# Attention, token mixer and two MLPs on one core: small VectorE operations rewritten one column at a time

## The chip, the cores and the metric

The kernel runs on one core of a Trainium2 chip. A core has five engines that work side by side, each through its own list of instructions in order: TensorE (PE in the rows; its weight loads are PEld), VectorE (DVE), ScalarE (ACT), GpSimd (POOL) and SyncE (SP), which here issues the DMA transfers. The metric is the time on the device in microseconds, median of several runs.

## What is computed

The reference is a block-causal attention, then a token mixer and a channel MLP, then a second MLP behind a row normalization. Cut to what matters here:

```python
x = attention(q, k, v)                       # 4 x 576 rows of 512
u = x + token_mix(x)
x2 = u + relu(u @ moe_w_ch1) @ moe_w_ch2     # first MLP
mu  = mean(x2, axis=-1)                      # per row
var = mean((x2 - mu) ** 2, axis=-1)
xn  = (x2 - mu) / sqrt(var + 1e-06) * g_ln
out = x2 + relu(xn @ moe2_w_ch1) @ moe2_w_ch2
```

The MLP weights arrive as 64-bit floats. The kernel turns them into 32-bit floats, scales each matrix by a power of two, and splits weights and rows into two 16-bit planes; each product is then three 16-bit matmuls.

## The kernel before

Rows lie on the 128 partitions. The program has an attention stage (to about 240 us of the profile) whose steps stand in a table; after it `Mlps` works through the first MLP (to about 555 us), and `Pairs` through the second (from 527 us to the end), in three passes of 768 rows by four groups of hidden units. While the first MLP still runs, VectorE also decodes the weights of the second one (lines 945 to 952), ScalarE scales and splits them, GpSimd forms the sums and the low planes, and SP stores the planes to DRAM and loads them again for the passes.

From 240 us on a planner (`Plan`) sets the order at build time: each step has an engine, a cost and the steps it needs, and is emitted when its planned time comes. The costs in that table are constants of the program and are the same before and after. On the chip every engine then goes through its list in that order and waits on semaphores.

Three pieces of small work on VectorE belong to the change.

- `spread(s)` makes the maximum of a set of four weight blocks ready for `diagonal` (ScalarE, line 987) and `across` (TensorE, line 993). For ten of the sets it reduces four columns to one (line 968) and works on one column: line 975 masks and shifts, line 976 joins that with a bit of the original. For the four sets to which the gains `g_ln` belong it works on four columns (lines 979 to 981) and reduces at the end (line 982).
- `root()` adds the epsilon to the variances of two row blocks (line 1436, two columns), and ScalarE takes the square root (`power`, line 1439).
- `newton()` refines the inverse root: a reciprocal (line 1443) and four operations on two columns (lines 1444 to 1447). `normed` (line 1451) then normalizes 128 x 512 elements with the mean and the inverse root as scalars per partition.

There are nine such pairs of row blocks, three for each pass. Behind `normed`, GpSimd forms sums of rows (line 1459), ScalarE and GpSimd make the planes (lines 1475 and 1477), and SP issues the DMA that transposes them for TensorE (line 1481).

In the second MLP VectorE combines the results of the first product (lines 1583 to 1611, tiles mm, hid, u, h), makes the low planes (line 1594), and adds up the second product (line 1657, tile psy). TensorE's matmuls of the first product are line 1550, those of the second line 1637. Of the first MLP they are lines 1163 and 1196.

Of the kernel before, what the change touches and what calls it, by code (L numbers as in the profile page):

```python
# [14 lines left out]
I32 = mybir.dt.int32  # L15
AF = mybir.ActivationFunctionType
ALU = mybir.AluOpType
# [4 lines left out]
P = 128  # L22
# [764 lines left out]
class Mlps:  # L787
# [173 lines left out]
    def spread(self, s):  # L961

        nc, top = self.nc, self.mx[s]
        m1 = self.small([P, 1], "mx1", 3)
        g = self.gains(s)
        m = self.small([P, 4], "mxf", 3) if g else m1
        if not g:
            nc.vector.tensor_reduce(m1, top, axis=AX.X, op=ALU.max)
            top = m1
        mi, ti = m.bitcast(I32), top.bitcast(I32)  # L970
        if not g:
            t1 = self.small([P, 1], "mxt", 3)
            ti, m1 = m1.bitcast(I32), self.small([P, 1], "mxu", 3)
            mi = t1.bitcast(I32)
            nc.vector.tensor_scalar(mi, ti, 0x07FFFFFF, 3, ALU.bitwise_and, ALU.logical_shift_left)
            nc.vector.scalar_tensor_tensor(
                m1.bitcast(I32), ti, 0x40000000, mi, ALU.bitwise_and, ALU.bitwise_or)
        else:
            nc.vector.tensor_scalar(mi, ti, 0x07FFFFFF, 3, ALU.bitwise_and, ALU.logical_shift_left)
            nc.vector.scalar_tensor_tensor(mi, ti, 0x40000000, mi, ALU.bitwise_and, ALU.bitwise_or)  # L980
            nc.vector.tensor_tensor(m, self.ga4, m, ALU.mult)
            nc.vector.tensor_reduce(m1, m, axis=AX.X, op=ALU.max)
        self.mx[s] = m1

# [364 lines left out]
class Pairs:  # L1349
# [58 lines left out]
    def plan_rows(self, p, t):  # L1408
        m, nc, st, plan = self.m, self.nc, {}, self.m.plan
        js = (6 * p + 2 * t, 6 * p + 2 * t + 1)  # L1410
        if p == 0:
            a, x = (("xt0", "u1"), ("xr", "wt2"), ("xt0", "u1"))[t]
# [20 lines left out]
        def root():  # L1433
            va, st["r"] = m.small([P, 2], "va", 3), m.small([P, 2], "vr", 3)
            st["va"] = va
            nc.vector.tensor_scalar(va, st["mv"][:, :, 1], 1e-6, None, ALU.add)  # L1436

        def power():
            nc.scalar.activation(st["r"], st["va"], AF.Sqrt)

        def newton():
            va, r, t_ = st["va"], st["r"], m.small([P, 2], "vt", 3)
            nc.vector.reciprocal(r, r)
            nc.vector.tensor_tensor(t_, r, r, ALU.mult)
            nc.vector.tensor_tensor(t_, t_, va, ALU.mult)
            nc.vector.tensor_scalar(t_, t_, -2.0, 6.0, ALU.mult, ALU.add)
            nc.vector.tensor_tensor(r, r, t_, ALU.mult)

        def normed(i):
            x = st["x"][i]  # L1450
# [50 lines left out]
        for i in range(2):  # L1501
            add(f"stats{i}", "DVE", 0.9, lambda i=i: stats(i), *got[i])
        add("root", "DVE", 0.2, root)
        add("power", "ACT", 0.25, power, "root")
        add("newton", "DVE", 1.0, newton, "power")
        for i in range(2):
            add(f"normed{i}", "DVE", 0.5, lambda i=i: normed(i), "newton",
# [293 lines left out]
```

## Time and profile before

| | us |
|---|---|
| median of 3 runs | 913.77 (910.42 to 915.55) |
| the profiled execution | 907.16 |
| its span, first to last instruction | 905.4 |
| PE busy | 829.2 (92% of the span) |
| DVE busy | 736.2 (81%) |
| POOL busy | 513.9 (57%) |
| ACT busy | 503.7 (56%) |

The span is what the trace shows; 1.8 us of the execution lie around it. The mean granted clock of TensorE is 0.977 of full speed. Busy shares are means over stages with different limits, so the stages have to be read one by one.

### The profile page before, as it was taken

The page shows a single profiled execution, that of the slowest core. Times are in us where ns is not written, and L with a number is a line of the kernel's source. Part 1 is how long each engine was busy: PE and PEld are TensorE (multiplying, and loading weights), DVE is VectorE, ACT ScalarE, POOL GpSimd, SP SyncE. Part 2 cuts the span into 40 slices and gives each one's busy share as a digit, 9 for nine tenths or more (in the row PEclk, how much of TensorE's full clock was granted, in tenths as well). Part 3 has the DMA queues.
Part 4 walks back from the last instruction along what each step waited for, and adds up shares of the span by engine and source line. Part 5 has one row for each costly group of instructions (what it writes and reads, how often), then busy time and mean ns, then how long its engine had stood idle before and what let it go on. Part 6 is the DMA issues. An engine that isn't in the chain of part 4 may idle for free. (4 is left out here: it accounts for less than half of the span.)

```text
span 905.4 us, 18022 instructions
## 1 busy us (share of the span) xinstructions
PE 829.2 (92%) x6606; PEld 562.3 (62%) x6606; DVE 736.2 (81%) x1434; ACT 503.7 (56%) x1211; POOL 513.9 (57%) x505
## 2 busy tenths in 40 slices
PE   6778988889889999999999887998999899999995
PEld 4567877778744454445444353675777667777774
DVE  6999877989986887989899986689867787666776
ACT  6788886877665567555565544553434443344330
POOL 4778788598100345346658785486556654572224
PEclk9979998999899999999999999999999999999998
DMA  8999999999994732436546994659747667455522
GB/s 214 235 198 185 231 204 196 168 231 206 253 259 117 186 117 98 132 107 212 201 179 182 304 336 170 232 187 230 194 152 261 193 170 204 145 192 174 171 76 81
DMA packets 237993, 171.71 MB, mean 190 GB/s; under 512 B 184208, under 2 KB 204176, under 8 KB 237904
## 3 DMA queue, kind: packets, MB, share of 16 engines
q1 hardware_dynamic: 237904, 170.56, 70.9%
q8 instruction: 52, 0.85, 0.4%
q14 instruction: 37, 0.30, 0.1%
HBM read 102.50 MB, written 28.84 MB: 145 GB/s over the span
## 5 line engine op out<-in xcount | busy, mean ns | idle before, releaser
L1196 PEld LDWEIGHTS <-hid 128*128 128x128 f16 x648 | 63.3, 98 | 75.3 <-issue 1.0
L1196 PE MATMUL psy<-w,hid 128*128 128x512 f16 x432 | 95.7, 380 | 0.0
L1163 PEld LDWEIGHTS <-w 128*128 128x128 f16 x480 | 46.9, 98 | 52.4 <-issue 7.0
L1550 PEld LDWEIGHTS <-xr__4654 128*128 128x128 f16 x504 | 49.4, 99 | 34.8 <-issue 6.8
L1550 PE MATMUL mm<-big,xr__4654 128*128 128x384 f16 x336 | 64.8, 331 | 6.4 <-DVE hid L1583 4.3
L1561 POOL TENSOR_TENSOR acc<-u__4660,acc 128x384 f16<-128x384 f32 x36 | 32.9, 915 | 64.3 <-ACT acc L1557 64.2
L437 ACT ACTIVATE wide<-ps,nm 128x128 f32<-128x128 f32 (+3 forms) x128 | 65.8, 524 | 4.0 <-POOL hlA L461 2.0
L1550 PEld LDWEIGHTS <-wt__4653 128*128 128x128 f16 x504 | 49.2, 98 | 28.1 <-issue 3.7
L1550 PE MATMUL mm<-big,wt__4653 128*128 128x384 f16 x336 | 63.4, 326 | 3.3 <-DVE hid L1583 3.3
L1174 ACT ACTIVATE hid<-mm 128x512 f16<-128x512 f32 (+1 forms) x60 | 32.6, 549 | 53.7 <-PE mm L1163 53.5
L1637 PE MATMUL psy<-acc,acc 128*128 128x256 f16 x432 | 62.4, 273 | 0.0
L1203 POOL TENSOR_TENSOR acc<-acc,big 128x512 f32<-128x512 f32 x12 | 15.3, 1274 | 83.0 <-ACT big L1202 83.0
L461 POOL TENSOR_TENSOR hlA<-wide,hlA 128x1024 f16<-128x1024 f32 (+1 forms) x32 | 55.3, 1737 | 9.7 <-DVE hlA L457 6.8
L1557 ACT ACTIVATE xt<-mm 128x384 f16<-128x384 f32 x30 | 14.7, 490 | 80.9 <-DVE u__4660 L1611 64.4
L372 PE MATMUL ps<-kt 64*128 64x256 f32 (+3 forms) x384 | 51.7, 386 | 6.4 <-ACT wide L437 3.1
L414 DVE TENSOR_REDUCE mx<-ps 128x2 f32<-128x768 f32 (+3 forms) x64 | 50.5, 815 | 8.5 <-PE ps L377 8.4
L1637 PE MATMUL psy<-acc,xt 128*128 128x256 f16 x378 | 53.7, 273 | 3.1 <-ACT hid L1654 2.4
L1583 DVE TENSOR_TENSOR hid<-mm,hid 128x384 f32<-128x384 f32 x72 | 39.8, 552 | 17.4 <-PE mm L1550 11.6
L1637 PE MATMUL psy<-acc,w 128*128 128x256 f16 x378 | 50.1, 273 | 2.2 <-DVE w L1657 1.2
L1177 DVE SCALAR_TENSOR_TENSOR hid<-mm,hid 128x512 f16<-128x512 f32 (+1 forms) x60 | 37.3, 631 | 17.7 <-ACT hid L1174 17.4
L1637 PE MATMUL psy<-acc,wt__4655 128*128 128x256 f16 x324 | 44.8, 273 | 5.0 <-DVE big L1657 4.0
L1637 PEld LDWEIGHTS <-acc 128*128 128x128 f16 x432 | 42.2, 98 | 9.7
(288 smaller groups left out, 2326.6 us busy)
## 6 DMA issues: line engine op xcount, KB each, us to landing
raw<-in_moe_w_ch_dram SPq DMA_DIRECT2D x56, 512.0 KB, 3.9
acc<-w2d SPq DMA_DIRECT2D x84, 256.0 KB, 3.8
wt__4653<-w1d SPq DMA_DIRECT2D x12, 896.0 KB, 4.8
xr__4654<-w1d SPq DMA_DIRECT2D x12, 896.0 KB, 4.9
rawq<-in_q_dram SPq DMA_DIRECT2D x16, 256.0 KB, 3.2
rawq<-in_k_dram SPq DMA_DIRECT2D x16, 256.0 KB, 3.6
rawv<-in_v_dram SPq DMA_DIRECT2D x32, 128.0 KB, 3.7
u_dram<-u SPq DMA_DIRECT2D x8, 512.0 KB, 4.4
```

What stands on the lines that cost most here:

```text
L372: nc.tensor.matmul(views[hh], kt[r, a, KQ + t * P : KQ + (t + 1) * P], kt[r, c, KK : KK + n], start=i == 0, stop=False)
L414: nc.vector.tensor_reduce(s["mx"][:, c : c + 2], ps, axis=AX.X, op=ALU.max)
L437: nc.scalar.activation(d[:, g, sl], s["ps", key][:, g, sl], AF.Exp, scale=SCALE, bias=s["nm"][:, c + g : c + g + 1], accum_out=s["rs"][:, ...
L461: (nc.vector if last else on("l" + key)).tensor_tensor(lo_, src, hi, ALU.subtract)
L1163: self.nc.tensor.matmul(ps.rearrange("p (t n) -> p t n", n=P), W[:, a, h * P : (h + 1) * P], self.xt[b][:, :, 4 * c + k], start=i == 0, st ...
L1174: self.nc.scalar.activation(hid[:, 0, :w], ps, AF.Relu)
L1177: self.nc.vector.scalar_tensor_tensor(hid[:, 1, :w], ps, 0.0, hid[:, 0, :w], ALU.max, ALU.subtract)
L1196: self.nc.tensor.matmul(y, self.hid[v, h][:, a, k * P : (k + 1) * P], W[:, c], start=i == 0, stop=i == 11)
L1550: self.nc.tensor.matmul(ps[:, : self.W].rearrange("p (t n) -> p t n", n=P), w[:, i, j, a], x[:, :, at, j, c], start=first and n == 0, stop ...
L1561: self.nc.gpsimd.tensor_tensor(h[:, 1], src, h[:, 0], ALU.subtract)
L1583: add(k, "DVE", 0.55, lambda: dve.tensor_tensor(ps(src) if out is None else T[out], ps(src), T[x], ALU.add), 0)
L1637: self.nc.tensor.matmul(ps, h[:, a, t * P : (t + 1) * P], self.w2[o][:, r, c], start=n == 0, stop=n == 5)
```

## The change

Each of the small operations is written as one instruction per column, 128 x 1 elements. Where the other operand was a tensor it is now a scalar per partition, a column of a tile. Line 976 becomes a tensor_scalar whose second operand is the column. The four-column form gets a tile of its own for the shifted words (mxt4). In `newton` the square of r and its product with the variance become one instruction with two scalars per partition. The reciprocal and the reduction stay as they were.

```diff
@@ spread @@
             mi = t1.bitcast(I32)
             nc.vector.tensor_scalar(mi, ti, 0x07FFFFFF, 3, ALU.bitwise_and, ALU.logical_shift_left)
-            nc.vector.scalar_tensor_tensor(
+            nc.vector.tensor_scalar(
                 m1.bitcast(I32), ti, 0x40000000, mi, ALU.bitwise_and, ALU.bitwise_or)
         else:
-            nc.vector.tensor_scalar(mi, ti, 0x07FFFFFF, 3, ALU.bitwise_and, ALU.logical_shift_left)
-            nc.vector.scalar_tensor_tensor(mi, ti, 0x40000000, mi, ALU.bitwise_and, ALU.bitwise_or)
-            nc.vector.tensor_tensor(m, self.ga4, m, ALU.mult)
+            t4 = self.small([P, 4], "mxt4", 2)
+            cols = [[x[:, k : k + 1] for k in range(4)] for x in (ti, t4.bitcast(I32), mi, m)]
+            for t_, c, _, _ in zip(*cols):
+                nc.vector.tensor_scalar(
+                    c, t_, 0x07FFFFFF, 3, ALU.bitwise_and, ALU.logical_shift_left)
+            for t_, c, w, _ in zip(*cols):
+                nc.vector.tensor_scalar(w, t_, 0x40000000, c, ALU.bitwise_and, ALU.bitwise_or)
+            for k in range(4):
+                w = cols[3][k]
+                nc.vector.tensor_scalar(w, w, self.ga4[:, k : k + 1], None, ALU.mult)
             nc.vector.tensor_reduce(m1, m, axis=AX.X, op=ALU.max)
@@ root, newton @@
-            nc.vector.tensor_scalar(va, st["mv"][:, :, 1], 1e-6, None, ALU.add)
+            for i in range(2):
+                nc.vector.tensor_scalar(
+                    va[:, i : i + 1], st["mv"][:, i, 1:2], 1e-6, None, ALU.add)
...
-            va, r, t_ = st["va"], st["r"], m.small([P, 2], "vt", 3)
-            nc.vector.reciprocal(r, r)
-            nc.vector.tensor_tensor(t_, r, r, ALU.mult)
-            nc.vector.tensor_tensor(t_, t_, va, ALU.mult)
-            nc.vector.tensor_scalar(t_, t_, -2.0, 6.0, ALU.mult, ALU.add)
-            nc.vector.tensor_tensor(r, r, t_, ALU.mult)
+
+            nc.vector.reciprocal(st["r"], st["r"])
+            t2 = m.small([P, 2], "vt", 3)
+            cols = [[x[:, i : i + 1] for i in range(2)] for x in (st["va"], st["r"], t2)]
+            for va, r, t_ in zip(*cols):
+                nc.vector.tensor_scalar(t_, r, r, va, ALU.mult, ALU.mult)
+            for va, r, t_ in zip(*cols):
+                nc.vector.tensor_scalar(t_, t_, -2.0, 6.0, ALU.mult, ALU.add)
+            for va, r, t_ in zip(*cols):
+                nc.vector.tensor_scalar(r, r, t_, None, ALU.mult)
```

The lists of TensorE, ScalarE, GpSimd and SP are the same before and after, with the same waits. On VectorE only the instructions shown change. First, VectorE at a set with gains in the first MLP (lines 979 to 982 of before), with the neighbours on its list; L1177 and L1205 read TensorE's results. Before:

```order
L952 SCALAR_TENSOR_TENSOR raw_75<-raw_75,word 128x512
L1177 SCALAR_TENSOR_TENSOR hid_4391<-mm,hid_4391 128x512
L979 TENSOR_SCALAR mxf<-mx_6390 128x4
L980 SCALAR_TENSOR_TENSOR mxf<-mx_6390,mxf 128x4
L981 TENSOR_TENSOR mxf<-ga_4839,mxf 128x4
L982 TENSOR_REDUCE mx_6565<-mxf 128x1
L1205 SCALAR_TENSOR_TENSOR acc_3917<-psy,rs,acc_3917 128x512
```

The same place of VectorE's list now; the lines behind the change have higher numbers, so that 1184 is the old 1177 and 1212 the old 1205:

```order
L1184 SCALAR_TENSOR_TENSOR hid_4391<-mm,hid_4391 128x512
L982 TENSOR_SCALAR mxt_6587<-mx_6410 128x1 x4
L985 TENSOR_SCALAR mxf<-mx_6410,mxt_6587 128x1 x4
L988 TENSOR_SCALAR mxf<-mxf,ga_4839 128x1 x4
L989 TENSOR_REDUCE mx_6585<-mxf 128x1
L1212 SCALAR_TENSOR_TENSOR acc_3917<-psy,rs,acc_3917 128x512
```

Three instructions of four columns became twelve of one. Second, VectorE at the last pair of row blocks of the third pass, whose rows are made ready at 725 us of the profile: va is the variance, vr the inverse root, and the other rows combine TensorE's results. Before:

```order
L1657 SCALAR_TENSOR_TENSOR hid_4390<-psy,rg,hid_4390 128x512
L1436 TENSOR_SCALAR va<-mv 128x2
L1657 SCALAR_TENSOR_TENSOR hid_4391<-psy,rg,hid_4391 128x512
L1594 SCALAR_TENSOR_TENSOR wt__4655<-mm,wt__4655 128x384
L1443 RECIPROCAL vr<-vr 128x2
L1444 TENSOR_TENSOR vt<-vr 128x2
L1445 TENSOR_TENSOR vt<-vt,va 128x2
L1446 TENSOR_SCALAR vt<-vt 128x2
L1447 TENSOR_TENSOR vr<-vr,vt 128x2
L1583 TENSOR_TENSOR mm<-mm,hid_4386 128x384
```

The same place of VectorE's list now (1670, 1607 and 1596 are the old 1657, 1594 and 1583):

```order
L1670 SCALAR_TENSOR_TENSOR hid_4390<-psy,rg,hid_4390 128x512
L1444 TENSOR_SCALAR va<-mv 128x1 x2
L1670 SCALAR_TENSOR_TENSOR hid_4391<-psy,rg,hid_4391 128x512
L1607 SCALAR_TENSOR_TENSOR wt__4655<-mm,wt__4655 128x384
L1452 RECIPROCAL vr<-vr 128x2
L1456 TENSOR_SCALAR vt<-vr,va 128x1 x2
L1458 TENSOR_SCALAR vt<-vt 128x1 x2
L1460 TENSOR_SCALAR vr<-vr,vt 128x1 x2
L1596 TENSOR_TENSOR mm<-mm,hid_4386 128x384
```

One instruction became two at L1436, and four became six behind the reciprocal; their neighbours stand where they stood.

## Rows read from the trace of the kernel before

**Rows 1.** Page, part 2: busy tenths of PE in 40 slices of 22.6 us.

```profile
PE   6778988889889999999999887998999899999995
```

**Rows 2.** Windows, DVE on tiles mxf, vt, then L1436, L976: window, us, busy (count), ....

```profile
240.00:740.00 500.00, 7.94 (x16) 0.99 0.64 195
...
240.00:740.00 500.00, 15.51 (x36) 0.99 0.64 195
...
240.00:740.00 500.00, 5.92 (x9) 0.99 0.64 195
...
240.00:740.00 500.00, 5.25 (x10) 0.99 0.64 195
```

**Rows 3.** Timeline of POOL and DVE: start, us, instruction, [idle before it].

```profile
613.73 0.92 POOL L1561 TENSOR_TENSOR acc<-u__4660,acc 128x384 f16<-128x384 f32 x1 [0.76 <-ACT acc L1557]
613.75 0.15 DVE L1443 RECIPROCAL vr<-vr 128x2 f32<-128x2 f32 x1
613.94 0.72 DVE L1444 TENSOR_TENSOR vt<-vr 128x2 f32<-128x2 f32 x1
...
615.48 2.12 POOL L1477 TENSOR_TENSOR w<-u__4659,w 128x1024 f16<-128x1024 f32 x1
615.57 2.05 DVE L1446 TENSOR_SCALAR vt<-vt 128x2 f32<-128x2 f32 x1
```

**Rows 4.** One-column instructions: by tile (ns min/median/max), then timeline of DVE, POOL.

```profile
L975 DVE TENSOR_SCALAR mxt<-mx x10: 153/153/154, 240.7 to 561.5; 128x1 int32<-128x1 int32 x10
...
513.77 0.15 DVE L1001 TENSOR_SCALAR wi<-wt 128x1 int32<-128x1 int32 x1
...
513.85 0.14 DVE L1003 TENSOR_SCALAR ws<-wt 128x1 int32<-128x1 int32 x1
...
514.11 0.73 POOL L1460 TENSOR_TENSOR u__4660<-acc,acc 128x256 f32<-128x256 f32 x1
514.15 0.21 DVE L1026 TENSOR_SCALAR rg<-wi 128x1 f32<-128x1 f32 x1
```

**Rows 5.** Timeline of DVE, PE and ACT, 463 to 544 us.

```profile
463.58 0.69 DVE L1177 SCALAR_TENSOR_TENSOR hid<-mm,hid 128x512 f16<-128x512 f32 x1 [0.51 <-ACT hid L1174]
...
504.59 1.79 DVE L976 SCALAR_TENSOR_TENSOR mxu<-mx,mxt 128x1 int32<-128x1 int32 x1
...
506.87 0.22 PE L993 MATMUL mm<-diag,ones 128*128 128x128 bf16 x1 [2.46 <-ACT diag L987]
...
529.45 0.67 ACT L896 ACTIVATE raw<-raw 128x512 f32<-128x512 f32 x1 [3.38 <-DMA raw<-in_moe_w_ch_dram]
...
543.96 1.14 PE L1550 MATMUL mm<-big,wt__4653 128*128 128x384 f16 x6 [3.28 <-DVE hid L1583]
```

**Rows 6.** Windows: us, then busy of PE, PEld, DVE, ACT, POOL; PEclk, DMA, GB/s.

```profile
508.00:512.00 4.00, 4.00 (x12) 1.51 (x11) 3.23 (x10) 1.27 (x2) 0.59 (x1) 0.57 1.00 210
610.00:635.00 25.00, 20.52 (x156) 15.04 (x155) 22.77 (x42) 10.00 (x23) 15.18 (x16) 1.00 0.90 221
```

**Rows 7.** Timeline of DVE and PE around 562 us.

```profile
561.67 1.14 DVE L976 SCALAR_TENSOR_TENSOR mxu<-mx,mxt 128x1 int32<-128x1 int32 x1
...
563.33 2.99 PE L1550 MATMUL mm<-big,xr__4654 128*128 128x384 f16 x9 [3.16 <-DVE hid L1583]
```

**Rows 8.** Timeline of DVE: the normalization at 581 us, a product at 626 us.

```profile
581.37 0.90 DVE L1451 TENSOR_SCALAR x__4657<-x__4657,mv,vr 128x512 f32<-128x512 f32 x1
...
626.74 2.05 DVE L1445 TENSOR_TENSOR vt<-vt,va 128x2 f32<-128x2 f32 x1
```

**Rows 9.** Timeline of DVE and PE, 708 to 734 us.

```profile
708.74 1.58 DVE L1444 TENSOR_TENSOR vt<-vr 128x2 f32<-128x2 f32 x1
...
717.97 0.82 PE L1637 MATMUL psy<-acc,wt__4655 128*128 128x256 f16 x6 [1.02 <-DVE big L1657]
...
725.71 2.06 DVE L1436 TENSOR_SCALAR va<-mv 128x2 f32<-128x2 f32 x1
...
733.73 1.15 PE L1550 MATMUL mm<-raw,xr__4654 128*128 128x384 f16 x6 [0.92 <-DVE xt L1594]
```

## The prediction

> **What bounds the kernel now.** I read the slices of the page first, then the waits of TensorE, then the timeline of VectorE and GpSimd at the lines of the change. The slices show that TensorE is at nine tenths or more from 270 to 500 us and again from 725 us nearly to the end; between them it falls to 7 or 8 tenths in a few slices, at 498 to 566, 611 to 634 and 701 to 724 us [rows 1]. Only there can a faster VectorE shorten the program: in the full stretches a stall on VectorE is covered by matmuls. So the worth of the change has to be read place by place, not from VectorE's busy time.
>
> Next, the small operations. Their lines are busy for 7.94, 15.51, 5.92 and 5.25 us, 34.62 us in 71 instructions [rows 2]. That is 0.49 us each, for one to four columns. A one-column operation on the same engine takes 153 to 154 ns in all ten cases [rows 4]. Had all 71 taken 0.155 us they would be busy 11.0 us, so 23.6 us are stall. The timeline shows what they stall on: the reciprocal at 613.75 us starts while GpSimd runs and takes 0.15 us; the tensor_tensor behind it, also on two columns, ends at 614.66 us, with GpSimd's instruction (613.73 + 0.92 = 614.65); the tensor_scalar at 615.57 us lasts 2.05 us and ends at 617.62 us, again just as GpSimd does (615.48 + 2.12 = 617.60) [rows 3]. Reading: operations with two tensors from SBUF, and tensor_scalars from SBUF to SBUF on two columns, wait until GpSimd's running instruction ends; others pass.
>
> **The change part by part.** It makes all of these one column wide, with scalars for second tensors. A one-column tensor_scalar with constants has no stall in ten cases. With a scalar from a tile there is a case right under a running GpSimd instruction (514.11 to 514.84 us): line 1026 at 514.15 us takes 0.21 us [rows 4]. I take it that the new forms do not wait, and that all 23.6 us go.
>
> Added are 63 instructions: three in each of the 9 norm sets, nine in each of the 4 sets with gains. Two operations that don't need each other start 0.08 us apart (513.77 and 513.85) [rows 4]; one that needs the result before it starts 0.19 us after it (613.75 and 613.94) [rows 3]. So 63 cost 5.0 to 12.0 us. Columns of one step don't need each other, so I take 5.0. A scalar from a tile costs 0.06 us more (0.21 against 0.15) [rows 4]; there are 6 such reads per norm set, 8 per set with gains, and 10 at line 976: 96, or 5.8 us. Together 10.8 us on VectorE (bounds 5.0, if the reads are hidden, and 17.8), against 23.6 gone. Per norm set it is 0.6, per set with gains 1.2, at line 976 0.06 us.
>
> There is a rule that speaks against such a rewrite. The Trainium skill, page "VectorE: DVE Perf Modes", section "The DRAIN you can't avoid", says that after every operation the pipeline is flushed before the next one starts, and the page's rules advise to keep the number of operations small. The two starts 0.08 us apart, with the first lasting 0.15 us, don't agree with a full flush between independent operations. By the rule the addition would be the upper end, 17.8 us, and places 3 to 5 below would lose about 0.3 us each.
>
> What of it lies on TensorE's path, in five places; durations are those of the profiled execution:
>
> *Place 1, 504 us.* TensorE waits 2.46 us at 506.87 for the diagonal that ScalarE builds from line 976, which lasted 1.79 us [rows 5]. Here 1.79 - 0.16 - 0.06 = 1.57 us go. VectorE has had no idle time since 463.58 us [rows 5] and in that stretch passed one set with gains, two norm sets and another root. At the mean stalls of rows 2 (1.4 per set with gains, 1.1 per norm set behind the reciprocal, 0.5 per root) that is 5.1 us, less 2.6 added: at least the 0.9 us missing from 2.46. So the wait goes whole. Behind it TensorE was granted 0.57 of its clock over 508 to 512 us [rows 6], part of it at 1.2 instead of 2.4 GHz, right after that idle stretch; 4 x 0.43 = 1.7 us more. Upper end 4.2 us. But TensorE's next wait, 3.28 us at 543.96, is for VectorE, behind ScalarE that stood 3.38 us at 529.45 for a weight load from DRAM [rows 5], with the DMA engines at a share of 1.00 [rows 6]. If that load comes no earlier, all of the 4.2 us becomes a longer wait there. Lower end 0. Some of the transfers ahead of the load hang on VectorE's normalization and do move; I take 2.0.
>
> *Place 2, 562 us.* TensorE waits 3.16 us for a product that stands right behind line 976 on VectorE, 1.14 us long [rows 7]. 1.14 - 0.16 - 0.06 = 0.9 us go. The upper end is 2.3, if the wait shortens enough that the slow matmuls behind it (9 in 2.99 us, against 6 in 1.14 at 543.96 [rows 5, 7]) run at speed; lower 0.5. I take 0.9.
>
> *Place 3, 610 to 635 us.* TensorE is idle for 25 - 20.52 = 4.5 us [rows 6]. VectorE stalls 0.72 - 0.16 and 2.05 - 0.16 us in one norm set [rows 3], 2.05 - 0.16 in the next [rows 8]. The first of these is only half won: behind the norm set stands line 1451, from SBUF to SBUF on 512 columns, which waits for GpSimd too (0.90 us at 581.37 [rows 8]), and GpSimd runs until 617.60 [rows 3]. I count 1.3 us for the first set (its products, line 1657, do move ahead) and 1.9 - 0.6 = 1.3 for the second: 2.6. Bounds 1.3 and 4.5.
>
> *Place 4, 708 to 718 us.* 1.58 - 0.16 - 0.6 = 0.8 us on VectorE, with a wait of TensorE of 1.02 us behind it [rows 9]: 0.8, bounds 0.3 and 1.0.
>
> *Place 5, 726 to 734 us.* The root is 2.06 us long; ScalarE's square root and what stands behind that wait for it. 2.06 - 0.16 - 0.08 less 0.6 for the set behind it is 1.2 us, of which TensorE's wait of 0.92 us [rows 9] can give 0.9; bounds 0.3 and 0.9.
>
> Elsewhere the stalls are covered by matmuls [rows 1] and worth nothing. The sum is 2.0 + 0.9 + 2.6 + 0.8 + 0.9 = 7.2 us, with ends at 0 + 0.5 + 1.3 + 0.3 + 0.3 = 2.4 and 4.2 + 2.3 + 4.5 + 1.0 + 0.9 = 12.9. After 735 us TensorE is full [rows 1], so what it has gained by then should reach the end. The profiled execution took 907.16 us, 6.6 below the median of 913.77; 7.2 us from the median give 906.6.
>
> **The rivals.**
>
> *Hidden after all.* Place 1 turns wholly into a longer wait at 544, and the others give their lower ends: 2.4 us, 911.4. For it: the load at 529 and the full DMA engines; each engine waits for the others in these stages. Against: at places 2, 4 and 5 the waiting instruction stands directly behind the stalled one.
>
> *All of it.* The load moves with VectorE, and the clock stays up behind places 1 and 2: 11 us or more, 902.8. For it: 2.46 us is a short wait, and VectorE has several us in hand before 504.
>
> *A scalar read waits as a tensor does.* If one column with a scalar from a tile waits for GpSimd, the change doesn't do what it says, and it waits more often: eight times instead of two in a set with gains, four times instead of three behind a reciprocal. At a mean stall per operation of (7.94 - 16 x 0.155) / 12 = 0.46 and (15.51 - 36 x 0.155) / 36 = 0.28 us [rows 2], a set with gains stalls 3.7 instead of 1.4 us, a norm set 1.1 as before less the 0.5 of the root, and 1.2 and 0.6 us of added work come on top. A set with gains is then 3.5 us longer; the one in the stretch up to 504 makes TensorE's wait there longer by about that, and the norm sets at places 3 to 5 are 0.1 us longer each: about 4 us and with the slow clock behind it 5, 918.8. It decides from the first case in which line 1456 or 1460 lasts as long as GpSimd's instruction. Against it: line 1026 [rows 4], but that is a single case.
>
> **How the numbers follow.** Forecast, some 5 to 9.5 us gained: 0.48, alone 904 to 909. All of it: 0.17. Hidden: 0.28. The scalar that waits: 0.05; something else that costs as much: 0.02. A measurement here can tell 0.5%, 4.6 us, from no change. Faster by more than that: 0.65, the first two. Within it: 0.28. Slower: 0.07. The range reaches from 902 (all of it, less a little) to 912.5 (hidden, with the spread of the runs).
>
> **What would show it.** Right: lines 982 to 988, 1444 and 1456 to 1460 at 0.15 to 0.27 us each, none as long as a GpSimd instruction; no wait of TensorE at line 1000 near 504; the waits at 563, 717 and 733 us and the idle time of 610 to 635 us shorter or gone; line 1464 (the old 1451) longer than before in some cases, since it now meets GpSimd. Wrong: a wait near 541 longer by what 504 gained; any of the new lines at 0.5 us or more.

## The result and the profile after

The changed kernel takes 899.31 us (median of 4 runs, 898.71 to 900.28), the kernel before beside it 914.39 (4 runs, 910.42 to 915.55): a ratio of 0.9844 with a 95% interval of 0.9814 to 0.9873. It is faster, as forecast, but by some 15 us instead of 7.2, and below the range. The two profiled executions, 907.16 and 900.28 us, lie only 6.9 us apart. So two things have to be found: whether each part did what was forecast, and where the other 8 us come from.

TensorE's totals and slices of the page after, which answer to [rows 1]:

```profile
PE 828.0 (92%) x6606; PEld 562.9 (63%) x6606; DVE 721.8 (80%) x1497; ACT 503.0 (56%) x1211; POOL 514.0 (57%) x505
...
PE   6778988888799999999999997899999999999995
```

The slices at 611 to 634 and 701 to 724 us, which stood at 8, 9 and 9, 8, are full; the dip at 540 to 565 us is still there.

The timeline of VectorE and GpSimd at the place of [rows 3]:

```profile
613.50 0.91 POOL L1574 TENSOR_TENSOR acc<-u__4660,acc 128x384 f16<-128x384 f32 x1 [0.77 <-ACT acc L1570]
613.52 0.15 DVE L1452 RECIPROCAL vr<-vr 128x2 f32<-128x2 f32 x1
613.71 0.46 DVE L1456 TENSOR_SCALAR vt<-vr,va 128x1 f32<-128x1 f32 x2
614.09 0.27 DVE L1458 TENSOR_SCALAR vt<-vt 128x1 f32<-128x1 f32 x2
614.27 0.33 DVE L1460 TENSOR_SCALAR vr<-vr,vt 128x1 f32<-128x1 f32 x2
614.38 0.91 POOL L1574 TENSOR_TENSOR w<-h__4656,w 128x384 f16<-128x384 f32 x1
614.52 0.74 DVE L1670 SCALAR_TENSOR_TENSOR hid<-psy,rg,hid 128x512 f32<-128x512 f32 x1
615.18 2.47 DVE L1464 TENSOR_SCALAR x__4658<-x__4658,mv,vr 128x512 f32<-128x512 f32 x1
615.25 2.12 POOL L1490 TENSOR_TENSOR w<-u__4659,w 128x1024 f16<-128x1024 f32 x1
```

GpSimd runs from 613.50 on, and VectorE passes under it: the set takes 614.52 - 613.52 = 1.00 us. In seven of the nine sets it is 1.00 to 1.01 us; behind the other two, at 507 and 577 us, VectorE stands idle before its next instruction. What waits now is the normalization, line 1464 (the old 1451), 2.47 us beside GpSimd's 2.12, as the prediction said.

Windows of VectorE, for tiles mxf and vt and lines 1444 and 976 as in [rows 2], and line 982, which now writes another tile:

```profile
240.00:740.00 500.00, 4.83 (x36) 0.98 0.65 197
...
240.00:740.00 500.00, 8.02 (x54) 0.98 0.65 197
...
240.00:740.00 500.00, 2.24 (x18) 0.98 0.65 197
...
240.00:740.00 500.00, 2.14 (x10) 0.98 0.65 197
...
240.00:740.00 500.00, 1.29 (x16) 0.98 0.65 197
```

Together 18.5 us in 134 instructions, against 34.6 in 71. The waits of TensorE from 300 to 740 us (what, for whom: us, times, longest):

```profile
PE mm L1563 <- DVE hid L1596: 7.9, 5, 3.0
PE psy L1650 <- ACT hid L1667: 2.3, 4, 0.8
PE mm L1563 <- DVE xt L1607: 2.1, 2, 1.1
PE psy L1650 <- DVE big L1670: 0.6, 1, 0.6
PE psy L1650 <- DVE hid L1670: 0.2, 1, 0.2
```

The wait for the diagonal, 2.46 us [rows 5], is gone. Its place is taken in part by what was feared. The timeline of TensorE:

```profile
505.84 0.22 PE L1000 MATMUL mm<-diag,ones 128*128 128x128 bf16 x1
...
538.72 1.14 PE L1563 MATMUL mm<-big,wt__4653 128*128 128x384 f16 x6 [1.77 <-DVE hid L1596]
542.84 2.08 PE L1563 MATMUL mm<-big,wt__4653 128*128 128x384 f16 x6 [2.98 <-DVE hid L1596]
...
563.48 2.84 PE L1563 MATMUL mm<-big,xr__4654 128*128 128x384 f16 x11 [2.23 <-DVE hid L1596]
```

And of ScalarE ahead of it:

```profile
528.63 0.67 ACT L896 ACTIVATE raw<-raw 128x512 f32<-128x512 f32 x1 [5.27 <-DMA raw<-in_moe_w_ch_dram]
```

ScalarE now stands 5.27 us for the weight load instead of 3.38, and TensorE waits 1.77 + 2.98 us near 540 instead of 3.28. At place 2, in these two executions, it is as forecast: 3.16 became 2.23 us, 0.93 less. Places 1 and 3 in windows, as in [rows 6]:

```profile
508.00:512.00 4.00, 4.00 (x21) 1.82 (x19) 3.28 (x17) 1.95 (x5) 1.00 (x2) 1.00 0.90 184
540.00:547.00 7.00, 4.17 (x12) 1.72 (x12) 3.15 (x6) 4.82 (x12) 5.85 (x10) 0.53 0.53 170
610.00:635.00 25.00, 23.82 (x182) 17.60 (x181) 22.99 (x53) 11.04 (x25) 17.93 (x19) 1.00 0.95 244
```

The slow clock behind place 1 is gone (1.00 instead of 0.57), but TensorE is granted 0.53, near the lower level of 1.2 GHz, at 540 to 547 us, behind the idle stretch that opened there. At place 3, 1.2 us of idle time are left of 4.5.

### The profile page after: what moved, and what is told of

Read it like the earlier page. It is cut to its first block, busy times and chain, and to the rows that moved or that the text cites. A ratio compares the mean times of both kernels' runs of the same rounds, so it can differ in the third digit from the quotient of the medians.

```text
span 898.5 us, 18086 instructions
## 1 busy us (share of the span) xinstructions
PE 828.0 (92%) x6606; PEld 562.9 (63%) x6606; DVE 721.8 (80%) x1497; ACT 503.0 (56%) x1211; POOL 514.0 (57%) x505
## 4 chain that ended last, share of the span: by engine, by line
PE 53%; DVE 15%; DMA 8%; POOL 6%; issue 4%; ACT 3%; DVEq 0%; SPq 0%; POOLq 0%; ACTq 0%
PE mm L1170 13%; PE psy L1203 12%; PE psy L1650 11%; PE mm L1563 11%; DMA ptB<-hlB 4%; PE mm L587 2%; DMA x__4657<-x_dram 1%; DVE hid L1596 1%; PE mm L610 1%; POOL hlA L461 1%; DMA ptA<-hlA 1%; PE ps L372 1%; DVE hid L1670 1%; DVE mm L1596 1%; DMA raw<-in_moe_w_ch_dram 1%
## 5 line engine op out<-in xcount | busy, mean ns | idle before, releaser
L414 DVE TENSOR_REDUCE mx<-ps 128x2 f32<-128x768 f32 (+3 forms) x64 | 50.4, 813 | 10.5 <-PE ps L377 10.3
L1670 DVE SCALAR_TENSOR_TENSOR hid<-psy,rg,hid 128x512 f32<-128x512 f32 x54 | 40.0, 744 | 9.9 <-PE psy L1650 9.3
```

What stands on the lines that cost most here:

```text
L414: nc.vector.tensor_reduce(s["mx"][:, c : c + 2], ps, axis=AX.X, op=ALU.max)
L1670: nc.vector.scalar_tensor_tensor(a, ps[:, 256 * new : 256 * n], r, a, ALU.mult, ALU.add)
```

## The experiments

To compare executions I take the time between the same matmuls of TensorE, found in each trace by their place in its list: the ones that start at 300.09 and at 590.01 us in the first profile of before, and the end. The second cut separates the set maxima and places 1 and 2 from places 3 to 5. Each row of the table is one profiled execution. The first interval is the attention stage and the first steps behind it; of the instructions changed, only some of the first on line 976 (from 241 us on) lie in it.

| kernel | to 300 | 300 to 590 | 590 to end | median of its runs (n) |
|---|---|---|---|---|
| before, 1st profile | 300.1 | 289.9 | 315.4 | 914.39 (4) |
| before, 2nd | 302.6 | 292.2 | 316.8 | 915.15 (12) |
| before, 3rd | 303.8 | 290.5 | 315.4 | 912.91 (8) |
| after, 1st | 301.7 | 288.1 | 308.7 | 899.31 (4) |
| after, 2nd | 310.5 | 288.0 | 309.0 | 904.95 (6) |
| after, 3rd | 302.9 | 286.9 | 309.0 | 901.55 (6) |
| norm sets only | 304.6 | 290.1 | 309.0 | 903.19 (6) |
| maxima only | 308.2 | 288.2 | 315.8 | 912.57 (12) |
| columns, two tensors | 304.5 | 290.8 | 313.8 | 909.21 (12) |
| eight operations more | 307.8 | 288.2 | 315.6 | 910.02 (12) |
| normalization on ScalarE | 304.7 | 290.7 | 310.0 | 906.19 (6) |
| before, GpSimd in pieces | 306.5 | 292.9 | 313.2 | 911.53 (12) |
| shorter newton | 308.2 | 285.2 | 308.0 | 902.18 (6) |
| shorter newton, pieces | 308.5 | 285.7 | 309.0 | 902.71 (6) |

**Both kernels again.** No edit.

> The kernel before, unchanged, profiled a second time. Theory A (the first profile of before was one of its shorter executions): its runs lie at 910 to 916 us, the new profiled execution is 3 us or more above the first one (907.16), and the extra time is found on TensorE between 498 and 740 us as longer waits at the five places of the prediction or as stretches at half clock behind them. Theory B (the extra time is not in the places): the extra lies in the attention stage, before 240 us, or is spread evenly, and the five places show the same waits as before within 1 us. Theory C (the median of before was high by chance): the new runs lie near 907.

> The kernel before, a third profile. From TensorE's matmul at 300 us to the end its first profile took 605.3 us and its second 609.0, the second with 2.3 us more at 530 to 570 and 1.3 us more at 622 to 640 us, each with a stretch at half clock behind a wait. Theory A (before has waits of about 3 us at 541, 560 and 629 us, and the half clock follows them in some executions, so that its typical run is 2 to 4 us longer than the first profile): 607 to 610 us in that part. Rival (the first profile is typical, the second not): 605 to 606 us.

> The changed kernel, profiled a second time. All theories: 898.5 to 900.5 us and a spread of the runs under 2 us. Theory A: the waits left on TensorE between 498 and 740 us agree with the first profile of it within 0.5 us each; theory B: they move about as much as those of before do.

> The changed kernel, a third profile. In two profiles of it the time from TensorE's matmul at 300 us to the end was 596.8 and 597.0 us, while that matmul itself came at 301.7 and 310.5 us. Theory A (the attention stage, which the change does not touch, sets the spread between runs): again 597 us from there to the end within 0.5 us, and the rest of the run's time, 300 to 311 us, in front of it; median of the runs 899 to 906 us. Rival (the stages of the change vary as well): the second part moves by 1 us or more.

Theory A for before was half right and then fell. The second profile has 3.7 us more behind 300 us, at 530 to 570 and at 622 to 640 us. The window at 622 to 645 us (columns as in [rows 6]) of the first profile of before:

```profile
622.00:645.00 23.00, 19.98 (x153) 14.82 (x152) 20.24 (x38) 10.25 (x21) 13.51 (x16) 1.00 0.72 192
```

The same window of the second profile:

```profile
622.00:645.00 23.00, 18.49 (x131) 13.15 (x130) 21.10 (x40) 8.51 (x19) 12.14 (x14) 0.93 0.79 215
```

Behind the same wait (3.02 and 3.04 us) the clock stayed up once and fell once. But the third profile has 605.9 us behind 300 us, as the first (605.3): the first was not unusual there. The places themselves do move between profiles of one kernel. From 504 to 520 us, around place 1, the three profiles of before take 16.0, 16.1 and 14.4 us, since in the third the granted clock stayed at 1.00 behind the same wait (2.50 us, 2.46 in the first); the three of after take 11.7 each. And at place 2 the third profile of before has no stall. The timeline of VectorE there:

```profile
567.71 0.16 DVE L976 SCALAR_TENSOR_TENSOR mxu<-mx,mxt 128x1 int32<-128x1 int32 x1
```

And of TensorE:

```profile
568.39 2.11 PE L1550 MATMUL mm<-big,xr__4654 128*128 128x384 f16 x12 [2.18 <-DVE hid L1583]
```

Line 976 met no GpSimd instruction, and TensorE's wait is 2.18 us without any change to the kernel, as short as after (2.23). The 0.9 us of place 2 are thus there to be won in two of the three profiles.

What moves from run to run is the column in front: 300 to 310 us over these fourteen executions, 301.7 and 310.5 in two of the same changed kernel. Behind 300 us the changed kernel takes 596.8, 597.0 and 595.9 us: 1.1 us of scatter, where theory A had allowed 0.5. The runs expected at 898.5 to 900.5 us came at 901.08 to 909.29 in the second set. The ratio measured in the second set of runs is 0.9890 (0.9861 to 0.9919), in the third 0.9864 (0.9834 to 0.9893).

**One part alone.** Each takes over one half of the diff shown ahead of the prediction and leaves the other as before: `root` and `newton`, or `spread`.

> Only root and newton in columns; the maxima (spread) as before. Between the two profiled executions TensorE gained 6.6 us from 590 us on, where the norm sets are (places 3 to 5), and 1.5 us net before. Theory A, with the gain lying mostly in the norm sets: 7 us or more of the 15 us, 905 to 908. Rival (the maxima carry what the profile does not show, since a long wait at place 1 brings TensorE's half clock): 2 to 5 us, 910 to 913.

> Only the maxima (spread: the sets with gains and line 976) in columns; root and newton as before. Theory A, gain mostly in the norm sets: 1 to 5 us, 910 to 914. Rival (the maxima carry what the profile does not show): 8 to 12 us, 903 to 907. If the two parts add, this and the norm sets alone make 15 us together.

The norm sets alone have a ratio of 0.9898 (0.9865 to 0.9932), the maxima alone 0.9999 (0.9973 to 1.0025). With 903.19 us the norm sets gained more than expected (905 to 908), and of the 1 to 5 us expected of the maxima the runs show nothing. From 590 us on the norm sets carry everything (309.0 like the whole change, 315.8 like before). From 300 to 590 us the maxima alone are at 288.2, as the whole change, but that is one profile, and the runs don't bear it out. From 300 us on the two parts gain 7.6 and 2.7 us on the mean of the three profiles of before (606.7), together 10.3, and the whole change 10.1. At place 1 either part is enough. With the norm sets alone, the timeline of VectorE:

```profile
506.69 2.09 DVE L976 SCALAR_TENSOR_TENSOR mxu<-mx,mxt 128x1 int32<-128x1 int32 x1
```

And of TensorE behind it:

```profile
509.26 0.22 PE L993 MATMUL mm<-diag,ones 128*128 128x128 bf16 x1 [0.39 <-ACT diag L987]
```

Line 976 stalls for 2.09 us as ever, yet TensorE's wait behind it is 0.39 instead of 2.46 us: the two norm sets earlier on the list, at 478 and 492 us of before, are 2.9 us shorter together (2.37 and 2.57 to 1.00 each), and that lead covers the stall.

**Width or second tensor?** The changed kernel, with tensors again, still by column:

```diff
-                nc.vector.tensor_scalar(t_, r, r, va, ALU.mult, ALU.mult)
+                nc.vector.tensor_tensor(t_, r, r, ALU.mult)
+            for va, r, t_ in zip(*cols):
+                nc.vector.tensor_tensor(t_, t_, va, ALU.mult)
...
-                nc.vector.tensor_scalar(r, r, t_, None, ALU.mult)
+                nc.vector.tensor_tensor(r, r, t_, ALU.mult)
```

> The changed kernel, but in newton the square, its product with the variance and the last product are one-column tensor_tensor operations with two tensors, eight instructions instead of six; width as in the changed kernel, second operand as in the kernel before. Theory A (a second tensor from SBUF waits for GpSimd's running instruction at any width): the sets at 478, 492, 613, 624 and 704 us last 2 to 4 us from the reciprocal to the next instruction instead of 1.00, and of the 6.7 us that TensorE gained from 608 to 740 us, 4 to 6.5 go again. Rival (the width of two columns was what waited): each set lasts 1.1 to 1.3 us, and the time is that of the changed kernel within 1 us from 300 us on.

The second set of place 3 in this kernel, on VectorE:

```profile
631.07 0.25 DVE L1456 TENSOR_TENSOR vt<-vr 128x1 f32<-128x1 f32 x2
631.27 2.13 DVE L1458 TENSOR_TENSOR vt<-vt,va 128x1 f32<-128x1 f32 x2
633.36 0.22 DVE L1460 TENSOR_SCALAR vt<-vt 128x1 f32<-128x1 f32 x2
```

GpSimd at the same time:

```profile
631.19 2.13 POOL L1492 TENSOR_TENSOR w<-w,w 128x1024 f16<-128x1024 f32 x1
```

One column wide, with two tensors, line 1458 takes 2.13 us for its two columns and ends at 633.40, 0.08 us after GpSimd (633.32). Theory A: the stall is back (313.8 against 309.0 us, 4.8 of 6.6 lost). Line 976 of before had shown the same: one column, two tensors, 1.79 us [rows 5]. The tensor_scalar with constants passes under GpSimd on one column (614.09 us in the changed kernel, above), where on two it took 2.05 us [rows 3]. So two tensors wait at one column as at two and four, and a tensor_scalar waits at two, four and 512 columns but not at one; three columns were not run. The Trainium skill, page "SBUF — State Buffer", section "SBUF: two separate sides", says of two tensors: a VectorE operation with two inputs from SBUF and a GpSimd operation that reads SBUF exclude each other, and the one that starts first keeps the other out for its whole length. These rows agree, with GpSimd first (631.19 before 631.27 us).

**VectorE's time put back as work.** The changed kernel with

```diff
+            pad = m.small([P, 8], "vp", 2)
+            for k in range(8):
+                va, r, _ = (c[k % 2] for c in cols)
+                nc.vector.tensor_scalar(pad[:, k : k + 1], r, r, va, ALU.mult, ALU.mult)
```

> The changed kernel with eight more one-column operations in each newton, two pointer scalars each, into a tile that nothing reads: VectorE works where it used to stall. Starts of such operations lie 0.19 us apart, so each set lasts 2.5 instead of 1.0 us. Theory A (what the change gives is VectorE's time at the sets of 613, 624, 704 and 722 us, about one for one): 1.0 to 1.5 us are lost at each of the last three, 0 to 1 at the first, 0 at the sets of 478, 492, 577 and 688 us and 0 to 4 at that of 507: from 300 us to the end 600 to 603 instead of 597 us. Rival (the gain came from GpSimd and DMA running undisturbed, not from VectorE's time): under 1.5 us lost.

The second set of place 3 in this kernel, on VectorE:

```profile
631.50 0.15 DVE L1452 RECIPROCAL vr<-vr 128x2 f32<-128x2 f32 x1
631.70 1.55 DVE L1458 TENSOR_SCALAR vp<-vr,va 128x1 f32<-128x1 f32 x8
633.16 0.45 DVE L1460 TENSOR_SCALAR vt<-vr,va 128x1 f32<-128x1 f32 x2
```

The eight hold VectorE's set up by 633.16 - 631.70 = 1.46 us, and from 590 us on the whole gain is lost (315.6). The loss was larger than expected, since five sets pay, not four: against the third profile after, 1.0 us at the set near 613, 1.4 at 624, 1.0 behind that of 692, 1.8 around 708 and 1.5 at 722. TensorE thus follows VectorE about one for one at these sets. That the loss equals the whole gain is partly chance, since the set near 692 us had no stall before and now costs 1.0 us. The rival, with under 1.5 us lost, fell; GpSimd, busy for 513.9 us before and 514.0 after, had not been held up by VectorE either.

**Shorter GpSimd instructions instead.** The kernel before, with

```diff
-                nc.gpsimd.tensor_tensor(lo_, src, hi, ALU.subtract)
+                for k in range(src.shape[1]):
+                    nc.gpsimd.tensor_tensor(lo_[:, k], src[:, k], hi[:, k], ALU.subtract)
```

> The kernel before, VectorE's operations as they were; on GpSimd the low planes of the normalized rows (line 1477) are formed in pieces of 256 elements (two of 256 for 512, four for 1024) instead of one instruction of up to 2.12 us. Theory A (a small VectorE operation waits only until GpSimd's running instruction ends): no operation of root or newton lasts longer than 0.95 us, the 2.05 us at 615 and 626 us, the 1.58 at 708 and the 2.06 at 725 us become 0.75 or less, and from 300 us to the end TensorE gains 2 to 5 us. Rival (it waits until GpSimd has nothing left to do): they stay at 2 us or more, and nothing is gained or 1 us is lost to the longer planes.

The same set in this kernel, on VectorE:

```profile
634.86 0.18 DVE L1444 TENSOR_TENSOR vt<-vr 128x2 f32<-128x2 f32 x1
635.07 0.59 DVE L1445 TENSOR_TENSOR vt<-vt,va 128x2 f32<-128x2 f32 x1
635.70 0.60 DVE L1446 TENSOR_SCALAR vt<-vt 128x2 f32<-128x2 f32 x1
636.33 0.59 DVE L1447 TENSOR_TENSOR vr<-vr,vt 128x2 f32<-128x2 f32 x1
```

Line 1445 waits 0.59 instead of 2.05 us [rows 8], and no operation of root or newton lasts longer than 0.84: only the running instruction counts. But each operation behind it, which had passed free, now meets a piece of its own, and the set still takes 2.17 us instead of 2.77 (626.33 to 629.10 us in the first profile of before). From 590 us on 2.2 us are gained; from 300 to 590 us the time is 0.7 us above the longest of before, and the sum from 300 us on, 606.1 us, is that of before, where theory A had 2 to 5 us gained. The ratio of the runs, 0.9958 (0.9935 to 0.9981), is faster than that; I can't say why, beyond the scatter of the first interval.

**What is late next.** The changed kernel with line 1464 on ScalarE:

```diff
-            nc.vector.tensor_scalar(
-                x, x, st["mv"][:, i, 0:1], st["r"][:, i : i + 1], ALU.subtract, ALU.mult)
+            nm = m.small([P, 1], "nm", 4)
+            nc.vector.tensor_scalar(
+                nm, st["mv"][:, i, 0:1], st["r"][:, i : i + 1], -1.0, ALU.mult, ALU.mult)
+            nc.scalar.activation(
+                x, x, AF.Identity, bias=nm, scale=st["r"][:, i : i + 1])
```

> The changed kernel with the normalization of 128 x 512 elements moved from VectorE to ScalarE (scale and bias per partition), one small operation on VectorE in front of it. On VectorE the 18 normalizations are at least 0.53 us and up to 2.47 us long, the longest ones behind GpSimd. Theory A (line 1464 is what is late next at 613 to 628 us): TensorE's two remaining waits there, 0.62 and 0.56 us, go, and VectorE's 0.53 us for each of the other sets helps a little: 1 to 3 us gained from 300 us on. Rival (ScalarE's own work, the planes and the products of the first MLP, is on the path instead): 0 to 4 us lost.

The timeline of TensorE in this kernel, where it waits longest:

```profile
539.74 2.08 PE L1566 MATMUL mm<-big,wt__4653 128*128 128x384 f16 x6 [3.09 <-ACT hid L1614]
549.14 1.86 PE L1566 MATMUL mm<-big,wt__4653 128*128 128x384 f16 x6 [3.32 <-DVE hid L1599]
```

The loss has the rival's size, 3 us before 590 and 1 after, but not quite its cause. TensorE now waits 3.09 us for ScalarE at 537 us, and ScalarE itself stood idle for 3.38 us until 538.13 us, for a weight load from DRAM that comes next on its list. Why that load comes later in this kernel was not followed.

**A shorter newton.** On the changed kernel:

```diff
-                    va[:, i : i + 1], st["mv"][:, i, 1:2], 1e-6, None, ALU.add)
+                    va[:, i : i + 1], st["mv"][:, i, 1:2], 1e-6, -2.0, ALU.add, ALU.mult)
...
-            nc.scalar.activation(st["r"], st["va"], AF.Sqrt)
+            nc.scalar.activation(st["r"], st["va"], AF.Sqrt, scale=-0.5)
...
-                nc.vector.tensor_scalar(t_, t_, -2.0, 6.0, ALU.mult, ALU.add)
-            for va, r, t_ in zip(*cols):
-                nc.vector.tensor_scalar(r, r, t_, None, ALU.mult)
+                nc.vector.tensor_scalar(r, t_, 6.0, r, ALU.add, ALU.mult)
```

> The changed kernel with newton cut to two operations per column: root forms -2 times the variance with epsilon in its one instruction, ScalarE's square root undoes that by its scale, and the last instruction adds 6 and multiplies by r. Four instructions instead of six, nothing left out. Eight more instructions had cost about one for one at five of the nine sets. Theory A (that slope holds downwards): a set lasts 0.8 instead of 1.00 us, and 0.5 to 1.2 us are gained from 300 us on: 595 to 596 us. Rival (what is left there is bound elsewhere): 596 to 597 us as in the changed kernel.

> Both together: the changed kernel with the shorter newton and GpSimd's low planes in pieces of 256 elements. What still waits for GpSimd on VectorE is the normalization, up to 2.47 us for 0.53. Theory A (that wait is still on TensorE's path at 613 to 628 us): it falls to 1.3 us or less, and a further 0.5 to 1.5 us are gained on the version with the shorter newton alone. Rival (GpSimd's planes become longer, 2.8 instead of 2.12 us for 1024 elements, and the transposing DMA and TensorE wait for them): 0.5 to 3 us lost against it.

The second set of place 3 with the shorter newton, on VectorE:

```profile
628.00 0.15 DVE L1452 RECIPROCAL vr<-vr 128x2 f32<-128x2 f32 x1
628.19 0.46 DVE L1456 TENSOR_SCALAR vt<-vr,va 128x1 f32<-128x1 f32 x2
628.56 0.33 DVE L1458 TENSOR_SCALAR vr<-vt,vr 128x1 f32<-128x1 f32 x2
628.81 0.56 DVE L1594 TENSOR_TENSOR mm<-mm,hid 128x384 f32<-128x384 f32 x1
```

A set takes 0.81 instead of 1.00 us, and from 590 us on 0.7 to 1.0 us go, as theory A has it; the further 1.7 us and more before 590 lie where the clock behind the waits near 540 differs from run to run, and I don't claim them. In the runs (0.9854 of before, 0.9825 to 0.9884) it can't be told from the change itself. The pieces on top bring nothing: the longest normalization is 1.08 us, but from 590 us on 1.0 us is lost again. From 300 us on the shorter newton has the least time of those tried, 593.2 us; by the medians of the runs it is not the first.

## Why the prediction was wrong in size

*The mechanism: right.* None of the new operations lasts as long as an instruction of GpSimd: lines 982 to 988, 1444 and 1456 to 1460 take 0.12 to 0.27 us each. Scalars from a tile didn't wait; second tensors did, at one column too. The stalls summed to 23.6 us and the busy time of these lines fell by 34.6 - 18.5 = 16.1, with 12.8 forecast.

*The added work: mis-sized.* I took 0.6 us per norm set, 3 instructions more and six scalar reads at 0.06 us each. A set of before that met no GpSimd instruction shows what it was:

```profile
729.27 0.15 DVE L1443 RECIPROCAL vr<-vr 128x2 f32<-128x2 f32 x1
729.46 0.16 DVE L1444 TENSOR_TENSOR vt<-vr 128x2 f32<-128x2 f32 x1
729.66 0.16 DVE L1445 TENSOR_TENSOR vt<-vt,va 128x2 f32<-128x2 f32 x1
729.86 0.17 DVE L1446 TENSOR_SCALAR vt<-vt 128x2 f32<-128x2 f32 x1
730.06 0.16 DVE L1447 TENSOR_TENSOR vr<-vr,vt 128x2 f32<-128x2 f32 x1
730.14 0.56 DVE L1583 TENSOR_TENSOR mm<-mm,hid 128x384 f32<-128x384 f32 x1
```

From the reciprocal to the next instruction 0.87 us, and 1.00 after: 0.13 us more behind the reciprocal. I had left out that four operations, each waiting for the one before, became three pairs, so that one step of 0.2 us fell away.

*Places 3 to 5: the first step that failed.* Forecast 2.6 + 0.8 + 0.9 = 4.3 us; from 590 us on it is 6.6 (315.4 to 308.7 and 309.0), the same in every profile with the norm sets in columns and no work added. By stretches (590 to 640, to 722, to 740 us) it is 3.5, 1.5 and 1.5. Of the 2.3 us missing, some 0.7 are the added work (0.47 too much deducted at place 3, 0.2 up to the cap at place 4). Another 1.1 is the cap itself: I let places 4 and 5 give one wait of TensorE each, 1.02 and 0.92 us, where both gave 1.5; there are further, shorter waits behind these, and VectorE's time is worth about one for one there, as the eight added operations showed. One of them, of TensorE in the kernel before:

```profile
735.52 0.81 PE L1637 MATMUL psy<-acc,xt 128*128 128x256 f16 x6 [0.64 <-DVE hid L1657]
```

The rest is a stall that I had left out at place 3, the root of before at 622 us:

```profile
622.62 0.88 DVE L1436 TENSOR_SCALAR va<-mv 128x2 f32<-128x2 f32 x1
```

It takes 0.27 us now (two columns), and with the 1.77 us of the set behind it (2.77 to 1.00) makes the 2.4 us that TensorE gained from 622 to 640 us. The set before it came as foreseen: 2.98 us shorter on VectorE (613.75 to 617.73 us of before, 1.00 now), but 1.0 on TensorE, since the normalization takes the wait over.

*Places 1 and 2: right in kind.* Forecast 2.9 together; from 300 to 590 us it is 1.8 between the first profiles and 3.2 between the means of three (290.9 and 287.7). At place 1 the upper end of 4.2 us was gained by 520 us between the first profiles (4.3), and 3.2 of it turned into waiting near 540, behind the load and partly at half clock. In the means of three it is 3.8 gained and 1.1 lost again by 570 us. At place 2 the forecast 0.9 us came where the stall was, in two profiles of before out of three.

*The sum and the range: the second step that failed.* Behind 300 us it is 606.7 to 596.6 us in the means of three profiles, 10.1 instead of 7.2 us. From the median of 913.77 that would have been 903.7, inside the range and near the second rival, "all of it". The other 5 us of the first result lie in front of 300 us, a stage that the prediction put at nothing: 899.31 less 596.6 and less the 1.8 us around the span leaves 300.9 us for the changed kernel, 914.39 less 606.7 and 1.8 leaves 305.9 for before. The profiles have 300 to 304 us there for the kernel before and 302 to 310 for the changed one, so they show no gain in front, and nothing of the change is in that stage but the first two instructions on line 976, at 241 and 277 us, which take 0.16 us each before. Some 2 us of the first result are luck: the later medians of the changed kernel lie 2 and 6 us higher, and over all runs on record the medians are 901.5 us (16 runs) and 914.6 (93 runs of before), 13 us apart and not 15. That leaves some 3 us beyond what the three profiles show from 300 us on. That the runs of the result met a short first stage is worked out by subtraction, not seen in their traces; why that stage varies by 10 us, and whether the change has any part in it, stays open. As for the range, its lower end of 902 lay 0.8 us below "all of it", where three runs of before had already spread over 5.1 us, and above 900.9, which the sum's own upper end of 12.9 us gives.

*The rivals.* "Hidden after all" fell: 10 us came through. "A scalar read waits as a tensor does" fell with the first rows. So did the 17.8 us of added work by the rule of the Trainium skill, page "VectorE: DVE Perf Modes", section "The DRAIN you can't avoid": 0.13 us more behind a reciprocal, not 2 x 0.19 + 6 x 0.06 = 0.74. The prediction quoted that rule without its exception, which the section states: an operation that is not held starts earlier. The rows agree with it: columns of one step start 0.06 to 0.19 us apart, while each lasts 0.12 to 0.27.

## What to carry to other kernels

Small operations on VectorE are worth reading one by one where GpSimd runs beside them: here a two-column operation of 0.16 us lasted up to 2 us, and one column with scalars per partition did not wait in any of the fourteen traces (0.28 us at most). Price added small operations by the starts of a chain of them, not by their durations, and price a gain on the engine in front by all the short waits behind it, one for one, until they are used up. Where runs of one kernel scatter by 10 us, compare the time between the same two instructions in each trace, and take the rest from many runs.

## What was not expected

Three spacings of independent one-column operations on VectorE: 0.19 us with two scalars from tiles (eight in 1.55 us), about 0.12 with one, and 0.06 to 0.12 with constants alone, while each lasts 0.27, 0.21 and 0.15 us. And a shorter blocker is not a cure: GpSimd's instruction of 2.12 us, cut into four, let VectorE's first operation off after 0.59 us and caught the next two.
